# A transformer block on one core: 32 more elements in the tile of keys and values, and where the tiles behind it begin

## The chip, the cores and the metric

The kernel runs on one core of one Trainium2 chip. The metric is the device time of one execution in microseconds (us); lower is better. The engines are named as in the profile: PE is TensorE (matrix multiply), PEld its loads of stationary operands, DVE is VectorE, ACT is ScalarE, POOL is GpSimd, and SP issues nearly all transfers.

## The reference

A block of a transformer over 2048 positions of width 640: a layer norm, attention of 32 heads of width 20 in which each position sees itself and seven earlier ones at a distance of 2, 4, ... 14, a projection and a residual; then a second layer norm and a gated feed-forward part of width 1728 with its residual. All inputs are float32.

```python
qkv = layernorm(x) @ wqkv                                  # 640 -> 3 * 640
logits[s, w] = q[s] . k[s - 2 * w] * 20 ** -0.5            # w = 0..7, masked below position 0
h = x + concat(softmax(logits) @ v[s - 2 * w]) @ wo
y = layernorm(h)
out = h + (silu(y @ w_gate) * (y @ w_up)) @ w_down
```

## The kernel before

The 2048 positions are cut into four batches (0 to 3) of 512. Each operand of a product is split into a high part (a cast to float32r on ACT) and a low part (a subtraction on DVE), and a product runs in three passes: high by high, high by low, low by high. A matmul of PE has two operands in the on-chip memory (SBUF): a stationary one of 128x128, which PEld loads just before, and a moving one of up to 512 columns. Nearly every matmul loads a new stationary operand.

The steps in the code, by the line of the matmul:

- L536, queries, keys and values (`qkv`): normalised activations are stationary, weights in `ra` moving. The activations of batches 0 and 2 lie in the tile `sha`, those of batches 1 and 3 in `shb`. Moving widths are 512 and 448, and 480 for the first two groups of batch 0.
- The attention itself (L600 to L647) runs on DVE, on products in the tile `pq`, with keys and values loaded into the tile `kv`.
- L724 and L1054, the projection: both operands in `ra`, 320 columns.
- L812, gate and up (`proj`): weights stationary (in `ra`, or late in the program in `wsl`), activations moving (in `shb`, or in `kv` for batch 3).
- L827, down (`down`): the gated activations, in the tile `acts`, are stationary for four of five output blocks with weights in `ra` moving; for the fifth the weights are stationary and `acts` moves.
- L977, a form of gate and up for batches 2 and 3 together (`pair_tile`), with sums of weights in `ra` or `wsl` stationary.

The order of each engine's instructions is written out by hand in a table (`ORDER`); nothing in it depends on addresses. The work of several steps is woven together: DVE does attention of later heads while PE does feed-forward products of batches 0 and 1.

The tiles come from one pool and lie one behind the other in each partition, in the order in which they are first asked for. Three pairs of names share one place: `pq` and `wsl`, `sha` and `h`, `st` and `acts`.

```python
FA_N = 3840 + 2560 + 32 + 128 + 128 + 2688
KV_N, PQ_N = 5280, 5120
RA_N = 19200
...
fa = sb.tile([128, FA_N], F32, name="fa")
ra = sb.tile([128, RA_N], F32R, name="ra")
shb = sb.tile([128, 5120], F32R, name="shb")
...
kv = sb.tile([128, KV_N], F32R, name="kv")
```

Elements have 4 bytes. The first tile, `fa`, begins at byte 16512 of each partition, behind a scratch area of 16384 bytes and four small constants of 32 bytes each. With the sizes above the built program has:

| Tile | first byte, before | remainder by 256 | elements |
|---|---|---|---|
| `fa` | 16512 | 128 | 9376 |
| `ra` | 54016 | 0 | 19200 |
| `shb` | 130816 | 0 | 5120 |
| `kv` | 151296 | 0 | 5280 |
| `pq` / `wsl` | 172416 | 128 | 5120 |
| `sha` / `h` | 192896 | 128 | 5120 |
| `st` / `acts` | 213376 | 128 | 3840 |

Within the tiles, operands of PE begin at multiples of 256 bytes, but for the 480-wide weights of the second group of batch 0, which begin 128 bytes past one. The attention reads `kv` up to element 5280, in three slots of 1760; later batch 3's activations take elements 0 to 5119. The lines that a step of the prediction needs besides:

```python
l = r_(XH + 128 * c, 128) if moved and a == 0 else t()[:, o : o + 128]            # qkv: t() is sha or shb
T.matmul(banks[bk][:, 0:n], l, r_(wq(g, w, c) + shift, n), ...)                   # L536: stationary, moving
T.matmul(banks[bk], ws(wt, gu + 1280 * w + wid * c + col, 128), x(a, c), ...)     # L812: ws is ra or wsl
T.matmul(banks[k], l, m, ...)                                                     # L827: one of l, m in acts
```

Of the kernel before, what the change touches and what calls it, by code (L numbers as in the profile page):

```python
# [186 lines left out]
def program(tc, x_in, wqkv_in, wo_in, ffn_in, ffl_in, const_in, out):  # L187
# [2 lines left out]
    P = Plan()  # L190

    FA_N = 3840 + 2560 + 32 + 128 + 128 + 2688
    KV_N, PQ_N = 5280, 5120
    RA_N = 19200

    with tc.tile_pool(name="sb", bufs=1) as sb, tc.tile_pool(
# [1086 lines left out]
```

## Time and profile before

| | us |
|---|---|
| median of 3 runs | 867.19 (866.93 to 868.58) |
| the profiled execution | 867.39 |
| its span, first to last instruction | 865.7 |
| PE busy (3977 matmuls) | 854.5 |
| PEld busy | 718.9 |
| DVE busy | 697.4 |
| ACT busy | 412.1 |

PE was granted 0.998 of its full clock. In the profile a matmul's tiles are written `out<-moving,stationary`: `bank<-ra,acts` is a matmul with weights of `ra` moving over a stationary block of `acts`. A matmul's own duration runs from its start to the end of its pipeline and overlaps the next one, so the rate at which matmuls follow each other is read from their starts. In the timeline a row joins successive instructions of one kind: its start, its length, the line, the tiles, and how many they are; the start of the next row ends the last step of a row.

### The profile page before, as it was taken

The page shows a single profiled execution, that of the slowest core. Times are in us where ns is not written, and L with a number is a line of the kernel's source. Part 1 is how long each engine was busy: PE and PEld are TensorE (multiplying, and loading weights), DVE is VectorE, ACT ScalarE, POOL GpSimd, SP SyncE. Part 2 cuts the span into 40 slices and gives each one's busy share as a digit, 9 for nine tenths or more (in the row PEclk, how much of TensorE's full clock was granted, in tenths as well). Part 3 has the DMA queues.
Part 4 walks back from the last instruction along what each step waited for, and adds up shares of the span by engine and source line. Part 5 has one row for each costly group of instructions (what it writes and reads, how often), then busy time and mean ns, then how long its engine had stood idle before and what let it go on. Part 6 is the DMA issues. An engine that isn't in the chain of part 4 may idle for free.

```text
span 865.7 us, 10685 instructions
## 1 busy us (share of the span) xinstructions
PE 854.5 (99%) x3977; PEld 718.9 (83%) x3977; DVE 697.4 (81%) x807; ACT 412.1 (48%) x722; POOL 3.3 (0%) x12
## 2 busy tenths in 40 slices
PE   7999999999989999999999999999999999999998
PEld 6888888889978888988888888788888888888886
DVE  5599999999999899998999899999667865553333
ACT  7766556432873434575433368444446333242331
POOL 0000000000000000000000000000000000000000
PEclk9999999999999999999999999999999999999999
DMA  6987786769697888649989977887752303362302
GB/s 199 280 239 197 233 256 161 214 199 249 181 298 248 268 270 290 194 116 300 322 269 274 308 247 197 255 300 260 259 160 87 127 22 98 115 205 88 107 30 92
DMA packets 86852, 177.75 MB, mean 205 GB/s; under 512 B 33408, under 2 KB 51584, under 8 KB 86032
## 3 DMA queue, kind: packets, MB, share of 16 engines
q1 hardware_dynamic: 85392, 176.41, 66.4%
q10 hardware_dynamic: 1408, 0.66, 0.3%
q8 instruction: 31, 0.51, 0.2%
q14 instruction: 21, 0.17, 0.0%
HBM read 132.07 MB, written 43.65 MB: 203 GB/s over the span
## 4 chain that ended last, share of the span: by engine, by line
PE 97%; ACT 1%; DVE 1%; DMA 1%; issue 0%; SPq 0%; ACTq 0%; DVEq 0%
PE bank L812 35%; PE bank L536 24%; PE bank L827 21%; PE bank L977 7%; PE bank L724 6%; PE bank L1054 2%; PE bank L392 1%; DMA fa<-in_x_dram 1%; PE bank L481 0%; PE bank L1161 0%; ACT L847 0%; ACT L618 0%; ACT ra L793 0%; ACT shb L395 0%; DVE fa L352 0%
## 5 line engine op out<-in xcount | busy, mean ns | idle before, releaser
L812 PE MATMUL bank<-shb,ra 128*128 128x512 f32 x1050 | 254.5, 393 | 1.6 <-ACT shb L395 1.2
L812 PEld LDWEIGHTS bank<-shb,ra 128*128 128x128 f32 x1050 | 197.5, 189 | 44.8 <-ACT shb L395 1.4
L827 PE MATMUL bank<-ra,acts 128*128 128x512 f32 x656 | 173.8, 396 | 0.0
L827 PEld LDWEIGHTS bank<-ra,acts 128*128 128x128 f32 x656 | 122.4, 188 | 26.8
L536 PE MATMUL bank<-ra,sha 128*128 128x512 f32 (+2 forms) x480 | 107.9, 382 | 0.3 <-ACT sha L483 0.3
L536 PE MATMUL bank<-ra,shb 128*128 128x512 f32 (+1 forms) x470 | 102.7, 378 | 0.0
L536 PEld LDWEIGHTS bank<-ra,sha 128*128 128x128 f32 x480 | 89.4, 188 | 14.5 <-ACT sha L483 0.6
L536 PEld LDWEIGHTS bank<-ra,shb 128*128 128x128 f32 x470 | 88.0, 188 | 12.6
L600 DVE TENSOR_TENSOR pq<-kv,pq 128x2560 f32<-128x2560 f32 x32 | 90.2, 2819 | 2.0 <-DMA kv<-ksc 1.6
L640 DVE TENSOR_TENSOR pq<-pq 128x1280 f32<-128x1280 f32 (+2 forms) x96 | 89.6, 933 | 2.3
L631 DVE TENSOR_TENSOR pq<-kv,pq 128x2560 f32<-128x2560 f32 x32 | 90.3, 2823 | 0.9
L605 DVE TENSOR_REDUCE pq<-pq 128x128 f32<-128x2560 f32 x32 | 90.0, 2813 | 0.4
L788 DVE TENSOR_TENSOR ra<-fa,ra 128x640 fp32r<-128x640 f32 x70 | 56.3, 819 | 27.8 <-ACT ra L778 25.0
L543 ACT ACTIVATE st<-bank,fa 128x480 f32<-128x480 f32 (+3 forms) x120 | 50.6, 474 | 57.1 <-PE bank L536 42.3
L778 ACT CAST ra<-fa 128x640 fp32r<-128x640 f32 x56 | 40.6, 726 | 61.2 <-PE bank L827 61.0
L793 ACT CAST ra<-fa 128x1280 fp32r<-128x1280 f32 (+1 forms) x41 | 50.1, 1221 | 24.1 <-PE bank L812 18.0
L841 ACT CAST acts<-fa 128x512 fp32r<-128x512 f32 x52 | 32.1, 619 | 57.6 <-DVE fa L848 43.7
L724 PE MATMUL bank<-ra 128*128 128x320 f32 x360 | 56.4, 309 | 0.0
L724 PEld LDWEIGHTS bank<-ra 128*128 128x128 f32 x360 | 54.3, 188 | 1.9 <-ACT fa L727 0.5
L847 ACT ACTIVATE fa<-bank 128x512 f32<-128x512 f32 x42 | 25.1, 598 | 62.3 <-PE bank L812 59.5
L848 DVE TENSOR_TENSOR fa<-bank,fa 128x512 f32<-128x512 f32 x42 | 28.8, 686 | 30.7 <-PE bank L812 21.3
L827 PE MATMUL bank<-acts,ra 128*128 128x512 f32 x164 | 45.9, 394 | 0.1
(161 smaller groups left out, 873.9 us busy)
## 6 DMA issues: line engine op xcount, KB each, us to landing
fa<-in_ffn_dram SPq DMA_DIRECT2D x47, 960.0 KB, 6.5
kv<-ksc SPq DMA_DIRECT2D x32, 440.0 KB, 6.0
kv<-vsc SPq DMA_DIRECT2D x32, 440.0 KB, 6.8
ra<-lsc SPq DMA_DIRECT2D x21, 640.0 KB, 6.3
lsc<-ra SPq DMA_DIRECT2D x13, 640.0 KB, 6.2
ra<-lsc SPq DMA_DIRECT2D x23, 320.0 KB, 5.6
ksc<-st SPq DMA_DIRECT2D x32, 160.0 KB, 3.7
pq<-qsc SPq DMA_DIRECT2D x16, 320.0 KB, 5.7
```

What stands on the lines that cost most here:

```text
L536: T.matmul(banks[bk][:, 0:n], l, r_(wq(g, w, c) + shift, n), start=(p, c) == first_mm, stop=(p, c) == last_mm)
L543: P.add("ACT", act(m) + 0.06, lambda: A.activation(stage_t()[:, o : o + NJ * m].rearrange("p (t j c) -> p t j c", j=NJ, c=w)[:, :, j, :], ...
L600: P.add("DVE", dve(2560), lambda: V.tensor_tensor(pq(PROD, 2560).rearrange("p (j w c) -> p j w c", j=2, w=W), window(ko, 2 * jp), pq(qo + ...
L605: P.add("DVE", dve(2560), lambda: V.tensor_reduce(pq(lo + 128 * jp, 128), pq(PROD, 2560).rearrange("p (n d) -> p n d", d=DH), axis=AX.X, o ...
L631: V.tensor_tensor(pq(PROD, 2560).rearrange("p (j n d) -> p j n d", j=2, d=DH), bass.AP(tensor=v.tensor, offset=v.offset, ap=[list(v.ap[0]) ...
L640: V.tensor_add(dst(v), v[:, :, 0:m, :], v[:, :, m : 2 * m, :])
L724: T.matmul(banks[bk][:, 0:320], l, r_(m, 320), start=p == 0 and c == 0, stop=p == 2 and c == NC - 1)
L788: P.add("DVE", tt(640), lambda o=o: V.tensor_sub(ws(t, lo + o, 640)[p0:], fa[p0:, raw + o : raw + o + 640], ws(t, hi + o, 640)[p0:].bitcas ...
L793: P.add("ACT", act(n), lambda: A.copy(ws(wt, gu, n), f(raw, n)), r=[rf(raw, n)], w=[rws(wt, gu, n)], prio=PR["fh"])
L812: T.matmul(banks[bk], ws(wt, gu + 1280 * w + wid * c + col, 128), x(a, c), start=p == 0 and c == 0, stop=p == 2 and c == NC - 1)
L827: T.matmul(banks[k], l, m, start=first and p == 0, stop=stop and p == len(passes) - 1)
L977: T.matmul(banks[bk], ws(wt, o + 2048 * w + 128 * k, 128), xv_[k](a), start=first and p == 0 and k == 0, stop=stop and p == 2 and k == n - ...
```

## The change

The tile `kv` gets 32 elements (128 bytes) more at its end. Nothing reads or writes them. The program has the same instructions, in the same order on each engine.

```diff
     FA_N = 3840 + 2560 + 32 + 128 + 128 + 2688
-    KV_N, PQ_N = 5280, 5120
+    KV_N, PQ_N = 5312, 5120
     RA_N = 19200
```

What differs is where the three places behind `kv` begin; all ahead of them stay.

| Tile | first byte, after | remainder by 256 |
|---|---|---|
| `pq` / `wsl` | 172544 | 0 |
| `sha` / `h` | 193024 | 0 |
| `st` / `acts` | 213504 | 0 |

`fa` still begins 128 bytes past a multiple of 256. The last tile ends at byte 228864 of each partition.

## The prediction

> **What bounds the kernel now.** I began with the page: the busy times and the chain that ended last.
>
> ```profile
> PE 854.5 (99%) x3977; PEld 718.9 (83%) x3977; DVE 697.4 (81%) x807; ACT 412.1 (48%) x722; POOL 3.3 (0%) x12
> ...
> PE 97%; ACT 1%; DVE 1%; DMA 1%; issue 0%; SPq 0%; ACTq 0%; DVEq 0%
> ```
>
> PE is 97% of the chain and busy for 854.5 us. Whatever alters the rate at which matmuls follow each other reaches the end, unless another engine stops PE; whatever alters a transfer does not, since transfers are 1% of the chain. The next question is where another engine could stop PE. The busy times by stretch tell that (the columns are the stretch, its length, PE, PEld, DVE, ACT, POOL, then clock and transfers):
>
> ```profile
> 40.00:250.00 210.00, 207.54 (x1016) 182.04 (x1015) 201.90 (x195) 117.33 (x263) 0.00 (x0) 0.99 0.79 219
> 250.00:600.00 350.00, 349.49 (x1631) 292.12 (x1631) 328.50 (x336) 170.81 (x254) 0.73 (x2) 1.00 0.83 262
> 600.00:866.00 266.00, 261.84 (x1169) 214.98 (x1167) 146.41 (x231) 94.39 (x145) 1.35 (x3) 1.00 0.35 115
> ```
>
> Three stretches with different limits. Up to 250 us DVE has 8.1 us free out of 210 and is as full as PE. From 250 to 600 PE is busy for all but 0.5 us and DVE has 21.5 us free. After 600 DVE is free for 120 us and PE alone counts.
>
> **What the change does to a matmul.** No instruction is added, removed or moved. Three places begin 128 bytes later, on a multiple of 256 bytes. So the only question is whether an instruction's time depends on that, and this trace holds the comparison, since `ra`, `shb` and `kv` stand on such multiples already and `wsl`, `acts` and `sha` do not. Here are five successive rows of PE's timeline in batch 3: the same line, the same moving tile, the stationary block once in `wsl` and once in `ra`.
>
> ```profile
> 776.43 2.49 PE L812 MATMUL bank<-kv,wsl 128*128 128x512 f32 x10
> 778.76 0.87 PE L827 MATMUL bank<-ra,acts 128*128 128x512 f32 x3
> 779.46 1.32 PE L812 MATMUL bank<-kv,wsl 128*128 128x512 f32 x5
> 780.62 2.44 PE L812 MATMUL bank<-kv,ra 128*128 128x512 f32 x10
> 782.89 0.40 PE L812 MATMUL bank<-kv,wsl 128*128 128x512 f32 x1
> ```
>
> From start to next start, ten steps with `wsl` take 778.76 - 776.43 = 2.33 us, 233 ns each; ten with `ra` take 782.89 - 780.62 = 2.27 us, 227 ns each. Nothing waits in between. Longer rows say the same: 27 steps with `acts` stationary, then 40 with everything on a multiple, then 45 with `sha` stationary.
>
> ```profile
> 844.53 6.42 PE L827 MATMUL bank<-ra,acts 128*128 128x512 f32 x27
> 850.79 0.85 PE L827 MATMUL bank<-acts,ra 128*128 128x512 f32 x3
> ```
>
> ```profile
> 475.70 9.24 PE L812 MATMUL bank<-shb,ra 128*128 128x512 f32 x40
> 484.77 1.56 PE L827 MATMUL bank<-ra,acts 128*128 128x512 f32 x6
> ```
>
> ```profile
> 117.99 10.70 PE L536 MATMUL bank<-ra,sha 128*128 128x512 f32 x45
> 128.53 0.60 PE L392 MATMUL bank<-fa 128*128 128x128 f32 x4
> ```
>
> They give (850.79 - 844.53) / 27 = 231.9 ns, (484.77 - 475.70) / 40 = 226.8 ns and (128.53 - 117.99) / 45 = 234.2 ns (one late start may be in the last). A step with an operand 128 bytes past a multiple of 256 costs 5.0 to 6.2 ns more than one without; I take 5.5.
>
> A fourth kind of step gains without being touched: aligned ones just behind the others.
>
> ```profile
> 644.98 1.31 PE L812 MATMUL bank<-shb,ra 128*128 128x512 f32 x5
> 646.13 0.87 PE L827 MATMUL bank<-ra,acts 128*128 128x512 f32 x3
> ```
>
> Five aligned steps that follow a few with `acts` take 1.15 / 5 = 230 ns, 3.2 ns above the 226.8 of a long aligned row. The slower rate seems to be carried on for some steps.
>
> The load of the stationary block is no longer for `wsl` than for `ra`:
>
> ```profile
> L812 PEld LDWEIGHTS bank<-kv,ra 128*128 128x128 f32 x135 | 25.3, 188 | 5.5
> L812 PEld LDWEIGHTS bank<-kv,wsl 128*128 128x128 f32 x120 | 22.6, 188 | 5.3
> ```
>
> Both take 188 ns, which lies inside a step of 227. So the extra time shows in the spacing and not in the load's own duration, and I can't say where in PE it arises. [...]
>
> **How many steps.** The matmuls that read `acts` and `wsl`, by stretch (PE first; two rows of `acts`, for the two later stretches, then one of `wsl`, which is used after 600 alone):
>
> ```profile
> 250.00:600.00 350.00, 113.22 (x434) 80.62 (x434) 20.31 (x30) 25.55 (x46) 0.10 (x1) 1.00 0.83 262
> 600.00:866.00 266.00, 97.57 (x387) 72.38 (x386) 17.77 (x26) 21.27 (x38) 0.00 (x0) 1.00 0.35 115
> ```
>
> ```profile
> 600.00:866.00 266.00, 60.77 (x243) 45.77 (x243) 12.31 (x15) 10.26 (x11) 0.10 (x1) 1.00 0.35 115
> ```
>
> And those with `sha`, by width, beside the narrow ones with `shb`:
>
> ```profile
> L536 PE MATMUL bank<-ra,shb 128*128 128x448 f32 x230 | 47.9, 365 | 0.0
> ...
> L536 PE MATMUL bank<-ra,sha 128*128 128x512 f32 x180 | 43.2, 397 | 0.0
> L536 PE MATMUL bank<-ra,sha 128*128 128x448 f32 x180 | 38.2, 367 | 0.0
> ...
> L536 PE MATMUL bank<-ra,sha 128*128 128x480 f32 x120 | 27.1, 382 | 0.3 <-ACT sha L483 0.3
> ```
>
> - Before 250 us: 180 wide steps with `sha` x 5.5 ns = 1.0 us. For the narrow ones the busy time per matmul is 38.2 / 180 = 212.2 ns with `sha` and 47.9 / 230 = 208.3 with `shb`, which bounds the gain by 3.9 ns; the mean durations, 367 and 365, point lower, and half of the 480-wide ones keep a misplaced moving operand. Zero would be the other bound. I take 1.7 ns x 300 = 0.5 us. Together 1.5 us.
> - From 250 to 600: 434 x 5.5 ns = 2.4 us.
> - After 600: 386 x 5.5 = 2.1 us with `acts` (one of the 387 is cut by the border and counted ahead of it) and 243 x 5.5 = 1.3 us with `wsl`: 3.5 us unrounded.
> - Aligned steps behind others: 5 x 3.2 ns = 16 ns for each return. Were each group of three down matmuls alone, 820 of them would make 273 returns and 4.4 us; were they all in rows like the 27, 30 returns and 0.5 us. The rows shown have three, six and twenty-seven; I take 80 returns, 1.3 us, half of it in each of the two later stretches.
>
> PE's steps thus shrink by 1.5 + 2.4 + 3.5 + 1.3 = 8.7 us in all.
>
> **What arrives at the end.** After 600 us nothing stands against PE: 3.5 + 0.65 = 4.1 us arrive in full. From 250 to 600 PE gains 3.0 us, and DVE, with 21.5 us free, has room, but its products are handed over in a fixed order and some come just in time; I let four fifths arrive, 2.4 us. Before 250 DVE is as full as PE, and a faster PE mostly waits for it: a quarter of 1.5, 0.4 us. The sum is 6.9 us. The profiled execution's 867.39 us becomes 860.5; the median of the runs, 867.19, lies 0.2 lower, and so I say 860.3.
>
> Do the other engines' own instructions change? DVE's subtraction of one form into `ra` and into `wsl` (line, tiles, minimum, median and maximum ns):
>
> ```profile
> L788 DVE TENSOR_TENSOR ra<-fa,ra x70: 782/818/832, 241.6 to 852.2; 128x640 fp32r<-128x640 f32 x67, 64x640 fp32r<-64x640 f32 x3
> ...
> L788 DVE TENSOR_TENSOR wsl<-fa,wsl x9: 816/822/826, 736.6 to 811.2; 128x640 fp32r<-128x640 f32 x9
> ```
>
> 818 against 822 ns: at most half a per cent, so I count nothing for DVE.
>
> **The rivals.** *DVE takes back all that PE gains before 600 us.* For it: DVE is 96% busy up to 250 and 94% from there to 600. Against it: in the middle stretch PE stands still for 0.5 us only, so DVE is nearly always ahead. Then 4.1 us arrive: 863.1.
>
> *Nothing changes.* The slow steps would be slow for their place in the program (short groups, changing banks) and not for their address. The interleaved `kv,wsl` and `kv,ra` rows speak against it, and so does `sha`, which differs from `shb` in nothing but the batch. Then 867.2. [...]
>
> *Slower: DVE's attention suffers from the new place of `pq`.* Keys and values in `kv` begin on a multiple of 256, `pq` until now did not. If a DVE instruction lost time when its two sources begin alike, it would be here:
>
> ```profile
> 40.00:250.00 210.00, 170.74 (x125) 2.92 (x7) 0.99 0.79 219
> 250.00:600.00 350.00, 238.88 (x178) 3.77 (x9) 1.00 0.83 262
> ```
>
> These are the instructions on `pq`, 409.6 us of DVE in the two stretches where it is nearly full. The late 4.1 us are outweighed from 4.1 / 409.6 = 1.0% on, if all of DVE's loss reaches PE; at 2% it would be 8.2 - 4.1 = 4.1 us slower, 871.3. The `wsl` row, whose two sources begin alike (`fa` and `wsl` are both 128 past), shows 0.5% where the other shows none, less than half of that point.
>
> **How the numbers follow.** The forecast has a chance of 0.62; that all 8.7 us arrive 0.06 (858.5); that DVE takes the early gain 0.22; no change 0.06; slower 0.04. The low end takes everything: 8.7 us, 0.9 more at 6.2 ns a step on 1243 wide steps, and 0.6 more for aligned steps: 857.0. The high end is DVE's rival at 5.0 ns on the 629 late steps without any followers: 3.2 us, 864.0. About 1 in 10 is left out on the slow side. This kernel's runs let 0.2%, 1.7 us, be told from no change: faster 0.9, same 0.06, slower 0.04.
>
> **What would show it.** In the trace after, rows of L827 with `acts` and of L812 and L977 with `wsl` should step at 227 ns, and short aligned rows behind them as well. PE's busy time should fall by 8 to 9 us, and PE's idle time should grow by about 2, around 240 us and before 600. DVE's instructions on `pq` should keep their 409.6 us. The prediction is wrong if the steps stay at 232 (then the address is not the cause), or if they fall and the end does not (then DVE bounds more than its free time shows).

## The result and the profile after

| | before | after |
|---|---|---|
| median of 4 runs each, us | 867.22 (866.93 to 868.58) | 858.97 (857.67 to 860.15) |
| profiled execution, us | 867.39 | 859.16 |
| its span, us | 865.7 | 857.4 |

The ratio is 0.9902 (95% interval 0.9884 to 0.9919): 8.3 us less, against a forecast of 860.3 in a range of 857.0 to 864.0.

The page's first part and the busy times by stretch, with the columns as above:

```profile
PE 845.8 (99%) x3977; PEld 718.0 (84%) x3977; DVE 696.7 (81%) x807; ACT 412.3 (48%) x722; POOL 3.3 (0%) x12
```

```profile
40.00:250.00 210.00, 207.50 (x1025) 182.61 (x1025) 202.01 (x196) 118.08 (x265) 0.00 (x0) 1.00 0.80 219
250.00:600.00 350.00, 349.37 (x1650) 294.38 (x1649) 332.38 (x339) 173.07 (x257) 0.73 (x2) 1.00 0.84 263
600.00:866.00 266.00, 253.62 (x1148) 211.16 (x1146) 142.39 (x228) 92.82 (x143) 1.35 (x3) 1.00 0.34 114
```

PE is busy 8.7 us less and DVE as long as before (696.7 against 697.4 us). In the middle stretch PE now does 1650 matmuls in the 350 us in which it did 1631, and it stands still no longer than before (0.6 us against 0.5). So nothing was handed back to a wait there.

PE's timeline, at the places shown of before:

```profile
769.80 2.43 PE L812 MATMUL bank<-kv,wsl 128*128 128x512 f32 x10
772.07 0.84 PE L827 MATMUL bank<-ra,acts 128*128 128x512 f32 x3
772.75 1.30 PE L812 MATMUL bank<-kv,wsl 128*128 128x512 f32 x5
773.88 2.43 PE L812 MATMUL bank<-kv,ra 128*128 128x512 f32 x10
776.15 1.30 PE L812 MATMUL bank<-kv,wsl 128*128 128x512 f32 x5
```

```profile
836.66 6.28 PE L827 MATMUL bank<-ra,acts 128*128 128x512 f32 x27
842.79 0.84 PE L827 MATMUL bank<-acts,ra 128*128 128x512 f32 x3
```

```profile
119.09 10.50 PE L536 MATMUL bank<-ra,sha 128*128 128x512 f32 x45
129.43 0.60 PE L392 MATMUL bank<-fa 128*128 128x128 f32 x4
```

From start to next start the ten steps with `wsl` take 227 ns each (233 before), the ten with `ra` 227 (227), the 27 with `acts` 6.13 / 27 = 227.0 (231.9), the 45 with `sha` 10.34 / 45 = 229.8 with a late start among them (234.2). The slow kind of step is gone.

**Time by stage.** All comparisons below use three marks of a profile: the start of the 45 matmuls with `sha` just shown (118.0 us before, 119.1 after), the first matmul of L812 and the first of L977, and the last of L827. The last three stand in PE's rows by line, which end in the first and the last start of a group. Of before and of after:

```profile
L812 PE MATMUL bank<-shb,ra x1050: 387/389/628, 246.8 to 663.2; 128*128 128x512 f32 x175
L827 PE MATMUL bank<-ra,acts x656: 387/393/483, 270.8 to 861.4; 128*128 128x512 f32 x164
...
L977 PE MATMUL bank<-shb,ra x45: 387/389/397, 665.5 to 731.1; 128*128 128x512 f32 x45
```

```profile
L812 PE MATMUL bank<-shb,ra x1050: 387/389/502, 247.2 to 658.7; 128*128 128x512 f32 x175
L827 PE MATMUL bank<-ra,acts x656: 387/389/482, 269.6 to 853.2; 128*128 128x512 f32 x164
...
L977 PE MATMUL bank<-shb,ra x45: 389/389/390, 661.0 to 725.3; 128*128 128x512 f32 x45
```

| kernel | `sha` mark to L812 | L812 to L977 | L977 to last L827 |
|---|---|---|---|
| before | 128.8 | 418.7 (clock of 0.50 for 3 us at its start) | 195.9 |
| e1, 64 longer | 128.8 | 417.3 | 195.8 |
| after | 128.1 | 413.8 | 192.2 |
| e3, `acts` off | 128.1 | 417.2 | 194.8 |
| e4, `wsl` off | 128.1 | 414.0 | 194.3 |
| e5, `sha` off | 128.8 | 413.8 | 192.3 |
| e2, `kv` off | 128.1 | 413.7 | 194.6 |
| e12, `kv` and `wsl` off | 128.1 | 413.8 | 194.5 |
| e9, all but `fa` off | 128.1 | 413.9 | 192.2 |

"Off" means 128 bytes past a multiple of 256. Where nothing that they read has changed place, the stages repeat to 0.1 or 0.2 us, while whole runs of one kernel spread over 1 to 6 us. In the profiles, what spreads is the start of the program and, in some executions, the first microseconds of L812: there PE's clock is granted at half speed for a varying time (0.50 from 12 to 14 us in after, 0.53 on average from 9 to 16 us in e5, and 0.50 from 247.5 to 250.5 us in before). Here are seven microseconds of the start, of after and of e9 (the clock is the third number from the end):

```profile
9.00:16.00 7.00, 5.81 (x22) 5.03 (x23) 4.18 (x8) 5.46 (x13) 0.00 (x0) 0.76 0.66 231
```

```profile
9.00:16.00 7.00, 6.92 (x37) 6.03 (x38) 3.48 (x7) 6.26 (x15) 0.00 (x0) 1.00 0.58 202
```

After does 22 matmuls there, e9 37. The profiled before had such a spell at L812's start instead (a clock of 0.60 from 246.7 to 251), which is why e1 is the better partner for the second stage. From e1 to after the three stages give 0.7 + 3.5 + 3.6 = 7.8 us. So the 8.7 us of busy time above are in part the clock's and no measure of the steps alone: from e1, whose profile has its slow spell at the start (a clock of 0.91 over the first 40 us), to after they would be 10.0 (855.8 and 845.8).

### The profile page after: what moved, and what is told of

It reads as the page before. It is cut to its first block, busy times and chain, and to the rows that moved or that the text cites. A ratio compares the mean times of both kernels' runs of the same rounds, so it can differ in the third digit from the quotient of the medians.

```text
span 857.4 us, 10685 instructions
## 1 busy us (share of the span) xinstructions
PE 845.8 (99%) x3977; PEld 718.0 (84%) x3977; DVE 696.7 (81%) x807; ACT 412.3 (48%) x722; POOL 3.3 (0%) x12
## 4 chain that ended last, share of the span: by engine, by line
PE 97%; ACT 1%; DVE 1%; DMA 1%; issue 0%; SPq 0%; ACTq 0%; DVEq 0%
PE bank L812 35%; PE bank L536 24%; PE bank L827 21%; PE bank L977 7%; PE bank L724 6%; PE bank L1054 2%; PE bank L392 1%; DMA fa<-in_x_dram 1%; PE bank L481 0%; PE bank L1161 0%; ACT L847 0%; ACT L618 0%; ACT ra L793 0%; ACT shb L395 0%; DVE fa L352 0%
## 5 line engine op out<-in xcount | busy, mean ns | idle before, releaser
L812 PE MATMUL bank<-shb,ra 128*128 128x512 f32 x1050 | 251.8, 390 | 1.7 <-ACT shb L395 1.2
L812 PEld LDWEIGHTS bank<-shb,ra 128*128 128x128 f32 x1050 | 196.2, 188 | 43.3 <-ACT shb L395 1.4
L827 PE MATMUL bank<-ra,acts 128*128 128x512 f32 x656 | 170.4, 391 | 0.0
L827 PEld LDWEIGHTS bank<-ra,acts 128*128 128x128 f32 x656 | 122.0, 188 | 24.1
L600 DVE TENSOR_TENSOR pq<-kv,pq 128x2560 f32<-128x2560 f32 x32 | 90.2, 2820 | 2.6 <-DMA kv<-ksc 2.2
L631 DVE TENSOR_TENSOR pq<-kv,pq 128x2560 f32<-128x2560 f32 x32 | 90.3, 2823 | 0.9
L827 PE MATMUL bank<-acts,ra 128*128 128x512 f32 x164 | 45.3, 391 | 0.1
```

The costliest lines, as they stand in the source:

```text
L600: P.add("DVE", dve(2560), lambda: V.tensor_tensor(pq(PROD, 2560).rearrange("p (j w c) -> p j w c", j=2, w=W), window(ko, 2 * jp), pq(qo + ...
L631: V.tensor_tensor(pq(PROD, 2560).rearrange("p (j n d) -> p j n d", j=2, d=DH), bass.AP(tensor=v.tensor, offset=v.offset, ap=[list(v.ap[0]) ...
L827: T.matmul(banks[k], l, m, start=first and p == 0, stop=stop and p == len(passes) - 1)
```

## The experiments

Theory A, the prediction's: an operand of PE that begins 128 bytes past a multiple of 256 makes its step slower, whichever operand it is. Rivals: the longer tile or the place in the program (N); the stationary operand alone (S); the difference between the places of the two operands (D). Every kernel starts from the changed one; a line that it inserts raises the line numbers behind it by one. Its ratio is to the kernel before.

**e1: longer still, but off again.**

```diff
-    KV_N, PQ_N = 5312, 5120
+    KV_N, PQ_N = 5344, 5120
```

> The tile of keys and values is 64 elements longer than before, so pq/wsl, sha/h and st/acts again begin 128 bytes past a multiple of 256. If the address makes the difference: the time of before, 867 us (ratio 0.998 to 1.002), and rows of L827 with acts step at 232 ns. If the longer tile itself or the greater distance to the tile ahead does: 859 us (0.990), steps of 227 ns.

868.03 us, ratio 1.0005 (0.9989 to 1.0021): the time of before. PE's timeline has the slow step again:

```profile
846.02 6.42 PE L827 MATMUL bank<-ra,acts 128*128 128x512 f32 x27
852.28 0.85 PE L827 MATMUL bank<-acts,ra 128*128 128x512 f32 x3
```

6.26 / 27 = 231.9 ns. N falls: the same program with a still longer tile is slow, so the address makes the difference.

**e2: `kv` alone off, which PE reads as the moving operand only.**

```diff
-    KV_N, PQ_N = 5312, 5120
+    KV_N, PQ_N = 5280, 5120
...
+        gap = sb.tile([128, 32], F32R, name="gap")
         kv = sb.tile([128, KV_N], F32R, name="kv")
```

> A gap of 32 unused elements ahead of the tile of keys and values, which has its old length; so only this tile begins 128 bytes past a multiple of 256, and PE reads it as the moving operand alone (L812 with kv x255, L977 with kv x60). If the place of either operand counts: the kv rows in batch 3 step at 232 ns and the time is 315 x 5.5 ns = 1.7 us over the changed kernel's 859 us, 860.7 (ratio 0.992). If the stationary operand alone counts: 227 ns, 859 us (0.990). If DVE suffers from kv's place, L600 and L631 take more than 2820 ns.

859.68 us, ratio 0.9925 (0.9902 to 0.9949). The time alone can't tell, the steps can:

```profile
768.86 2.48 PE L813 MATMUL bank<-kv,wsl 128*128 128x512 f32 x10
771.18 0.86 PE L828 MATMUL bank<-ra,acts 128*128 128x512 f32 x3
771.88 1.32 PE L813 MATMUL bank<-kv,wsl 128*128 128x512 f32 x5
773.03 2.49 PE L813 MATMUL bank<-kv,ra 128*128 128x512 f32 x10
775.36 1.33 PE L813 MATMUL bank<-kv,wsl 128*128 128x512 f32 x5
```

232 ns with `wsl`, 233 with `ra`, though both stationary blocks are on multiples of 256; and the last stage is 2.4 us longer than after's. S falls. DVE's products from `kv` keep their time (L631 at 2823 ns).

**e3, e4, e5: one place off at a time.**

```diff
 e3:  sb.tile([128, 5152], ..., tag="sha")   for sha and h: st/acts off
 e4:  KV_N, PQ_N = 5280, 5152                pq/wsl off
 e5:  KV_N, PQ_N = 5312, 5152, and e3's line sha/h off
```

> Only st/acts begin 128 bytes past a multiple of 256 (sha/h is 32 elements longer); pq/wsl and sha/h keep their multiples of 256. If the address costs 5.5 ns a step and is carried on by the steps behind: 820 x 5.5 = 4.5 us on PE and some 1.3 us of followers, 859 + 4 to 6 = 863 to 865 us (ratio 0.995 to 0.997); rows of L827 at 232 ns, rows of L812 with wsl in batch 3 at 227. If DVE had taken back what PE gained before 600 us, only the late half comes back: 859 + 2.1 to 2.8 = 861 to 862 (0.993).

> Only pq/wsl begin 128 bytes past a multiple of 256, as before the change; sha/h and st/acts keep their multiples of 256. By the address on PE: 243 x 5.5 = 1.3 us and up to 0.7 us of followers, 860.3 to 861.0 us (ratio 0.992 to 0.993), all of it after 600 us; rows with wsl at 232 ns, rows of L827 further away at 227. If DVE's products on pq gained from the change, the time before 600 us grows too, and L600, L605 and L631 take other than 2820, 2813 and 2823 ns.

> Only sha/h begin 128 bytes past a multiple of 256 (pq/wsl and sha/h are 32 elements longer). PE's steps at L536 with sha grow by 1.0 to 1.5 us in all, before 205 us. If DVE bounds the time up to 250 us, a quarter or less arrives: 859.0 to 859.4 us (ratio 0.990 to 0.991). If PE does: 860 to 860.5 (0.992). The start of the first L812 matmul shows it: at about 247.2 us, or 1 to 1.5 us later.

e3: 864.38 us, 0.9973 (0.9959 to 0.9987). e4: 861.28 us, 0.9941 (0.9923 to 0.9960). e5: 861.01 us, 0.9922 (0.9900 to 0.9944). By stages against after, `acts` costs 3.4 + 2.6 = 6.0 us, `wsl` 2.1 (all of it in the last stage; it is not read before, and 0.2 in the middle one is within what the stages repeat to) and `sha` 0.7 behind the mark. They sum to 8.8 where all three together cost 7.8, as they would if neighbours that carry a slow rate on were counted twice. e4 and e5, the steps with `wsl` and with `sha`:

```profile
771.14 2.50 PE L812 MATMUL bank<-kv,wsl 128*128 128x512 f32 x10
773.47 0.86 PE L827 MATMUL bank<-ra,acts 128*128 128x512 f32 x3
```

```profile
120.56 10.70 PE L536 MATMUL bank<-ra,sha 128*128 128x512 f32 x45
131.10 0.60 PE L392 MATMUL bank<-fa 128*128 128x128 f32 x4
```

233 and 234.2 ns, as before the change. e5 answers the question of DVE: from the mark to the first L812 it takes 0.7 us longer than after, and 120 wide steps with `sha` at 5.5 ns, the share of the 180 that lies behind the mark, are 0.66. All of it arrives, in the stretch where DVE is 96% busy. (L812's start itself, which I had meant to read, is 2.1 us later; 1.5 of that lies ahead of the mark, where the start spreads.) e3 answers it for the middle: 3.4 us come back between L812 and L977.

**e6, e7, e10, e11: 64, 192, 32 and 224 bytes past a multiple.**

```diff
-    KV_N, PQ_N = 5312, 5120
+    KV_N, PQ_N = 5328, 5120    (e6: 64; e7 has 5296: 192; e10 has 5320: 32; e11 has 5304: 224)
```

> The tile of keys and values is 48 elements longer than before, so the three places behind it begin 64 bytes past a multiple of 256. If a block of 512 bytes costs more whenever it does not begin on a multiple of 256: 232 ns a step with acts or wsl, 867 us (ratio 1.000). If the cost is graded by the distance: 228 to 230 ns, 861 to 865 (0.993 to 0.997). If only the bit of 128 bytes counts: 227 ns, 859 (0.990).

> The tile of keys and values is 16 elements longer than before, so the three places behind it begin 192 bytes past a multiple of 256, 64 bytes ahead of the next. If every remainder but zero costs the same: 232 ns a step, 867 us (ratio 1.000). If the cost is graded by the distance to a multiple: 228 to 230 ns, 861 to 865 us. If only the bit of 128 bytes counts: 232 ns, 867 us.

> The three places behind kv begin 32 bytes past a multiple of 256. With 64 past at 233.4 ns a step, 128 at 232.7 and 192 at 229 to 231, a cost that falls with the distance to the next multiple gives 233 to 235 ns here; a cost that needs some distance from the last multiple gives 227 to 230. One execution: 866 to 869 us or 858 to 863.

> The three places behind kv begin 224 bytes past a multiple of 256, 32 ahead of the next. A cost that falls with the distance to the next multiple gives 227.5 to 229 ns a step with acts or wsl stationary, 858 to 862 us; a cost that is the same for every block that crosses one more border of 256 bytes gives 231 or more, 864 to 867.

e6: 866.58 us, 0.9988 (0.9972 to 1.0003). e7: 862.85 us, 0.9947 (0.9922 to 0.9971). e10 and e11, one execution each: 871.6 and 868.0 us, both above the ranges that I had given, so only their steps are read. The 27 steps with `acts`, in this order (64, 192, 32, 224):

```profile
845.66 6.46 PE L827 MATMUL bank<-ra,acts 128*128 128x512 f32 x27
851.96 0.85 PE L827 MATMUL bank<-acts,ra 128*128 128x512 f32 x3
```

```profile
838.21 6.36 PE L827 MATMUL bank<-ra,acts 128*128 128x512 f32 x27
844.40 0.86 PE L827 MATMUL bank<-acts,ra 128*128 128x512 f32 x3
```

```profile
848.67 6.46 PE L827 MATMUL bank<-ra,acts 128*128 128x512 f32 x27
854.97 0.86 PE L827 MATMUL bank<-acts,ra 128*128 128x512 f32 x3
```

```profile
845.06 6.46 PE L827 MATMUL bank<-ra,acts 128*128 128x512 f32 x27
851.36 0.86 PE L827 MATMUL bank<-acts,ra 128*128 128x512 f32 x3
```

233.3, 229.3, 233.3 and 233.3 ns, beside 231.9 at 128 and 227.0 at 0. Every remainder tried but zero costs here, 192 the least. A cost that falls with the distance to the next multiple, which I had put up after e7, fails at 224; one of equal size for each crossed border fails at 192. The shape of the cost stays open.

**e8: `fa` on a multiple of 256 as well.**

```diff
-    FA_N = 3840 + 2560 + 32 + 128 + 128 + 2688
+    FA_N = 3840 + 2560 + 32 + 128 + 128 + 2688 + 32
...
+        gap = sb.tile([128, 32], F32, name="gap")
         fa = sb.tile([128, FA_N], F32, name="fa")
...
         AB2 = carve(2688)
+        carve(32)
```

> The changed kernel with 32 unused elements ahead of the first tile and 32 at its end, so that every tile begins at a multiple of 256 bytes, fa among them. What is left misplaced in the changed kernel are the 116 small products that read fa (L392, L481, L1161: steps of 108 to 109 ns, stationary and moving operand both in fa). If each gains 0 to 5 ns: 0 to 0.6 us, 858.4 to 859 us (ratio 0.9895 to 0.990), not to be told from the changed kernel. If DVE or ACT or transfers gain from fa's place, more than that.

859.53 us, ratio 0.9903 (0.9877 to 0.9930), not to be told from the changed kernel. `fa`'s place is worth nothing that these runs show.

**e9: all tiles but `fa` off, together.**

```diff
+        gap = sb.tile([128, 32], F32, name="gap")
         fa = sb.tile([128, FA_N], F32, name="fa")
```

> The changed kernel with 32 unused elements ahead of the first tile: fa now begins at a multiple of 256 bytes and every other tile, ra, shb and kv included, 128 bytes past one. So the stationary and the moving block of every matmul but those on fa begin alike. If each operand's own address counts: every 512-wide step takes 232 to 234 ns, 2840 x 5.5 = 15.6 us over the changed kernel, some 873 to 875 us (ratio 1.007 to 1.009). If only the difference between the two operands' places counts: 227 ns and 859 us (0.990).

859.27 us, ratio 0.9904 (0.9888 to 0.9921). By theory A this had to be the slowest kernel of all, and it is as fast as the changed one:

```profile
767.20 2.43 PE L813 MATMUL bank<-kv,wsl 128*128 128x512 f32 x10
769.46 0.84 PE L828 MATMUL bank<-ra,acts 128*128 128x512 f32 x3
770.14 1.30 PE L813 MATMUL bank<-kv,wsl 128*128 128x512 f32 x5
771.27 2.43 PE L813 MATMUL bank<-kv,ra 128*128 128x512 f32 x10
773.54 1.30 PE L813 MATMUL bank<-kv,wsl 128*128 128x512 f32 x5
```

226 ns with `wsl`, 227 with `ra`, every operand 128 bytes past a multiple. Theory A falls in that form; what counts is D, that the two operands have the same remainder by 256. By 512 they need not have: in the changed kernel `kv` begins 256 bytes past a multiple of 512 and `wsl` on one, and its `kv,wsl` rows step at 227 ns.

**e12: `kv` and `wsl` off, `ra`, `shb` and `acts` not.** The two theories differ here within one tile's work.

```diff
-    KV_N, PQ_N = 5312, 5120
+    KV_N, PQ_N = 5312, 5152
...
+        gap = sb.tile([128, 32], F32R, name="gap")
         kv = sb.tile([128, KV_N], F32R, name="kv")
```

> Of the tiles that PE reads only kv and pq/wsl begin 128 bytes past a multiple of 256; ra, shb, sha/h and st/acts keep their multiples. Each operand's own address says: every step with kv or wsl is slow, kv,wsl (x144), kv,ra (x171), shb,wsl (x45) and ra,wsl (x54) all at 232 to 233 ns, 414 x 5.5 = 2.3 us over the changed kernel, 861 us or more. The difference between the two operands' places says: kv,wsl at 227 ns although both are off, and kv,ra, shb,wsl and ra,wsl at 232 to 233 ns, 270 x 5.5 = 1.5 us and some followers, 860.5 to 861.5 us (ratio 0.992 to 0.993). The steps decide, the time does not.

860.91 us, ratio 0.9926 (0.9900 to 0.9952).

```profile
771.36 2.44 PE L813 MATMUL bank<-kv,wsl 128*128 128x512 f32 x10
773.64 0.85 PE L828 MATMUL bank<-ra,acts 128*128 128x512 f32 x3
774.33 1.31 PE L813 MATMUL bank<-kv,wsl 128*128 128x512 f32 x5
775.47 2.50 PE L813 MATMUL bank<-kv,ra 128*128 128x512 f32 x10
777.80 1.31 PE L813 MATMUL bank<-kv,wsl 128*128 128x512 f32 x5
```

Both operands off: 228 ns. One of them off: 233. The picture of before is turned round, where `kv,wsl` was slow and `kv,ra` fast. D holds, and the mix costs the last stage 2.3 us.

Whether the moving operand has to match its own stationary block or the next one, which is loaded during its step, shows where a row ends, in the starts of single steps of 512 columns from 40 us on (steps over 300 ns, which wait, left out). Such a place in the trace of before, with the load of the next block beside the last matmul ahead of it:

```profile
782.43 0.62 PE L812 MATMUL bank<-kv,ra 128*128 128x512 f32 x2
782.66 0.42 PEld L812 LDWEIGHTS bank<-kv,wsl 128*128 128x128 f32 x2
782.89 0.40 PE L812 MATMUL bank<-kv,wsl 128*128 128x512 f32 x1
```

The second of the two `kv,ra` matmuls starts at 782.66, the first load of `wsl` starts 3 ns behind it and lasts 188 ns; the step of that matmul takes 232 ns, where the nine ahead of it in the prediction's row take 226 to 230. Take steps with alike operands that follow at least four steps in which all is alike. In the profile of before, 1039 of them have a next stationary block that is alike too and take 227.2 ns on average; 73 stand just ahead of an unlike one and take 232.5. In e12 2097 take 227.0 and 22 take 232.7. So with a difference of 128 bytes an unlike next block is enough to slow a step whose own operands are alike. Whether an unlike block of its own is enough by itself is not shown: where the next block is alike, such a step always comes behind one that is unlike in both. Nor does this hold at every remainder: ahead of unlike blocks the same 73 steps take 226.7 ns at 64 and at 192 bytes, 235.2 at 32 and 234.3 at 224. Where in the step the time is lost stays open.

## Why the prediction was right, and where it was not

- *The change acts on PE's steps alone, by the address of the tiles.* Right: e1 undoes it with the address, and DVE's instructions on `pq` keep their durations (L600 2819 and then 2820 ns, L631 2823 both times).
- *A step with an operand 128 past a multiple costs 5.0 to 6.2 ns more.* The size was right, the rule behind it (theory A) was not. The trace of before holds no matmul of full width whose two operands are both off, and so "off" and "unlike the other" could not be told apart in it. Here they give the same kernel. For another, with all tiles off alike, the rule as I put it would forecast a gain where e9 shows none to be had.
- *Steps behind slow ones are slow.* Right, and of about the size taken. Matmul by matmul from L812 on, the order being the same in both, the first four wide alike steps behind unlike ones take 2.6 ns longer in e1 than in after and the next four 0.9; all followers together give 1.2 us where 1.3 were taken. It does not show in every row: ten `kv,ra` steps between rows with a slow `wsl` take 231 ns in e4 (775.33 to 777.64) but 227 before the change. And the five steps that stood for this in the prediction end just ahead of an unlike block, so their last one is slow for the reason that e12 shows.
- *PE's steps shrink by 8.7 us.* Measured 7.8 from e1 to after, behind the `sha` mark. In the second stage there are 515 steps with `acts`, 2.8 us at 5.5 ns, and half the followers' 1.3 makes 3.5: 3.5 measured. In the third, 305 with `acts` and 243 with `wsl`, 3.0 and 0.65: 3.7 against 3.6. `sha` was put at 1.5 us; 0.7 are seen, the wide steps behind the mark. The narrow ones' 0.5 us are not seen: the 448-wide steps take 205.3 ns before and 205.4 after. The 480-wide ones lie ahead of the mark, where the start's spread hides a gain; 92 in a row go from 217.1 to 214.6 ns on average, waits left out, but take 218.8 in e2, where `sha` is on a multiple too.
- *A quarter arrives before 250 us, four fifths up to 600.* This step failed. e5 and e3 show all of it arriving. I took a busy share of 94 to 96% for a bound, and called DVE as full as PE up to 250 us where the row had 8.1 us free for DVE and 2.5 for PE. DVE's instructions moved up along with PE's: measured from the start of the program, from e3 to after those of DVE gain 3.3 us between 252 and 658 us, and those of PE as much. Between 119 and 250 us DVE waits 1.5 us in after, for ACT alone; which hand-over lets it keep up was not followed further.
- *How near the number came.* 6.9 us were forecast to arrive and 7.8 are measured behind the mark. Two errors of opposite sign meet in that: PE's total was put 0.9 us too high, and 1.8 us of it were not let through. A slip has no weight: 629 steps at 5.0 ns are 3.1 us and not 3.2, and the end of the range stays 864.0.
- *The extra time shows in the spacing and not in the load's own duration.* Right: the loads of `wsl` for L812 with `kv` take 188 ns on average before and after. The place of the stationary block counts all the same: e12's two kinds of row differ in its remainder alone, and by 5 ns a step (228 and 233), and the step ahead of an unlike block, during which that block is loaded, is slow too (232.5 against 227.2 ns in the profile of before).

## What to carry to other kernels

Where PE bounds a kernel and each matmul loads a new stationary block, look at the remainder by 256 bytes of all its tiles: here tiles made alike took 5 to 6 ns off 512-wide steps of 232 to 233 and 8.3 us off 867.2, and 32 unused elements at the end of one tile bought it. Read the spacing of matmul starts within rows of one kind; a matmul's own duration overlaps the next one (a median of 389 ns for L827 in after, at steps of 227), and busy time takes in spells of a slower clock (from e1 to after it falls by 10.0 us, the stages by 7.8). And before a rule is drawn from a natural comparison in a trace, ask which second thing differs along with the first.

## What the runs showed of the hardware that was not expected

- In the rows of ten, 27 and 40 that are read above, the 512-wide step with a fresh stationary block takes 226 to 228 ns if both operands have the same remainder by 256 bytes, be it 0 or 128 (231 in e4's ten `kv,ra` steps between rows with a slow `wsl`), and 229 to 233 ns if not. At a difference of 128 bytes it is enough that the next block, loaded meanwhile, is unlike (232.5 against 227.2 ns in the profile of before).
- The 448-wide step with `sha` shows no such effect at 128 bytes (205.3 and 205.4 ns).
- DVE's products of 128x2560 (L600 and L631) show no such effect: they take 2819 to 2823 ns on average before, after and in e9, with `kv` and `pq` unlike (before) or alike (after and e9). ACT is busy 412.1 us before and 412.3 after.
- PE's clock was granted at half speed (0.50 from 12 to 14 us in after, and from 247.5 to 250.5 us before the change) in some executions in the first 16 us and behind the short stops of PE at about 247 us (1.2 us the longest). The stages that hold no such spell repeat to 0.1 or 0.2 us.
